# TensorE's matmuls in the program's order from the first step on, in a window-attention and Mish feed-forward kernel

## The chip, the cores and the metric

The kernel runs on one core of a Trainium2 chip. The metric is the device time of one execution in microseconds (us). Inputs and outputs are float32 in device memory.

## What is computed

Windowed attention over 8 sequences of 576 positions with 8 heads of 64, then a feed-forward layer whose activation is Mish, h * tanh(softplus(h)), on 4608 tokens of width 512 with an inner width of 2048:

```python
rel = pos[:, None] - pos[None, :]
mask = (rel >= 0) & (rel < 64)
scores = np.where(mask, scale * np.matmul(q, k.transpose(0, 1, 3, 2)), -1e9)
attn = np.exp(scores - np.max(scores, axis=-1, keepdims=True))
attn = attn / (np.sum(attn, axis=-1, keepdims=True) + 1e-09)
x = heads_side_by_side(np.matmul(attn, v))      # 4608 x 512
h = x @ w_in                                    # 512 x 2048
sp = np.where(h > 20.0, h, np.log1p(np.exp(np.minimum(h, 20.0))))
out = (h * np.tanh(sp)) @ w_out                 # 2048 x 512
```

## The kernel before

The 4608 tokens go in 12 chunks of 384 (`c`). A chunk's attention goes in four pairs of heads (`p`). Its feed-forward layer goes in 16 steps (`f`), each with 128 of the 2048 inner channels and its own weight tile.

**Attention of a pair.** `att_scores`: 12 small matmuls into two PSUM banks (`s_ps`); VectorE adds the mask and takes the row's extreme (L149), ScalarE takes the exponential (L152), VectorE scales by the sum (L160 to L162; in chunk 0 half by half, L156 to L158). `att_transpose`: six TensorE transposes of the probabilities `pr` into `t_ps` (L183), which are copied to `pT` (L184: by ScalarE, the second half by VectorE except in chunk 1). For chunks 4 and later VectorE and DMAs transpose instead, and TensorE has no part in it. `att_values`: 12 matmuls from `pT` into `o_ps`, whose result is split into a rounded part `xh` (ScalarE, L204) and the rest `xl` (VectorE, L205).

**A step.** `ffn_in`: 12 matmuls of 384 columns into `h_ps` (float32 products are built from rounded parts: xh and xl with the weight's high part, xh with its low part). VectorE clips (L223), ScalarE makes four passes (L224 to L231), VectorE combines with `h_ps` (L233), which frees the `h_ps` buffer (two exist). The result is split into `gh` (L235 or L237) and `gl` (GpSimd, L238). `ffn_out`, two steps later (`LAG`): 9 matmuls of 512 columns into three accumulators `acc`. The three accumulator banks (`ps_acc`) also hold `s_ps`, `t_ps` and `o_ps` of chunk 2's attention; other chunks mostly use three banks of their own (`bank`).

**Weights.** `load_w` fetches a step's weights as packed 64-bit words and takes them apart into float32 and then into a high and a low part: ScalarE L278, VectorE L279, L281, L282, L283, ScalarE L287, VectorE L288. There are two work buffers `wa`. A load's DMA waits until the tile three before it has been taken apart. All 16 tiles are taken apart once, while chunk 0 runs, and then stay.

**Order of the work.** The steps run (0, 0) to (0, 7), then chunks 0 and 1 in turns, then the rest of chunk 1, then chunk by chunk. Attention of chunk 0 comes first. Attention of a later chunk is spread over the steps before its own: `plan` gives each pair's scores, transposes and values a due time in half steps (`at`, `at + 0.6 * step`, `at + lag * step`), and the loop at L396 runs what is due (`run`) ahead of and behind each step's products. A scheduler then orders each engine's instructions by its own estimate of time and by priorities. `in_order()` takes part of that freedom away: inside it, every TensorE instruction that is traced is queued behind the last matmul recorded so far (`order[-1]`). It acts only once `ordered` holds something, which is from the first step of chunk 2 on (L401), and it is around the scores, the values and both products. The transposes are not recorded in `order` and are not inside it. On all engines the order is fixed when the program is built; at run time each engine takes its list from the top.

Of the kernel before, what the change touches and what calls it, by code (L numbers as in the profile page):

```python
# [27 lines left out]
def tile_window_attn_mish_ffn(  # L28
# [9 lines left out]
    nc = tc.nc  # L38
    NPAIR, _, NT = qT.shape
# [7 lines left out]
    NM = NB // 2  # L47
# [12 lines left out]
    ident = const.tile([P, P], F32, name="ident")  # L60
# [13 lines left out]
    for j in range(2):  # L74
        m = const.tile([P, P], F32, name=f"mask{j}")
# [15 lines left out]
    order = []  # L91
    ordered = []
# [4 lines left out]
    def in_order():  # L97
        return tc.issue_after(order[-1]) if ordered else nullcontext()
# [6 lines left out]
    def bank(c, p, name):  # L105
        if c == 2 or (c == 0 and p % 2 == 0):
            return ps_acc.tile([P, CH], F32, name=name, tag=next(sums))
        return ps_at.tile([P, CH], F32, name=name, tag="at")
# [56 lines left out]
    def att_transpose(c, p, pr):  # L165
        pT = next(pTs)
        if c > 3:


            moved = []  # L170
            tr = ap_.tile([P, P // 32, HM, 32], F32, name="tr", tag="pr", bufs=2)
            nc.vector.transpose(tr.rearrange("p k j i -> p j k i"),
                                pr.rearrange("p j (k i) -> p j k i", i=32))
            for r in range(0, P, 32):
                for k in range(0, P, 32):
                    if 0 <= k - r % BLK <= BLK:
                        moved.append(nc.sync.dma_start(pT[k:k + 32, r // 32, :, :], tr[r:r + 32, k // 32, :, :]))
            return pT, moved
        for h in range(2):
            t_ps = (bank(c, p, "t_ps") if c else ps_h.tile([P, CH], F32, name="t_ps", tag="h_ps")  # L180
                    ).rearrange("p (m k) -> p m k", k=P)
            for m in range(NM):
                nc.tensor.transpose(t_ps[:, m, :], pr[:, h * NM + m, :], ident)  # L183
            (nc.scalar.copy if h == 0 or c == 1 else nc.vector.tensor_copy)(  # L184
                pT[:, :, h * NM:(h + 1) * NM, :].rearrange("p r m i -> p m r i"),
                t_ps.rearrange("p m (r i) -> p m r i", i=32))
        return pT, []
# [19 lines left out]
    def ffn_in(c, x, f, alone=False):  # L207
        xh, xl = x
        h_ps = ps_h.tile([P, CH], F32, name="h_ps", tag="h_ps")
        n = 0  # L210
        for cc in range(NC_):
            for part, xx in ((0, xh), (0, xl), (1, xh)):
                pe(h_ps, ws[f][:, 0, part, cc * P:(cc + 1) * P], xx[:, cc, :],
                   start=n == 0, stop=n == 3 * NC_ - 1)
                n += 1
        t = mp.tile([P, CH], F32, name="t", tag="t", bufs=4)
        gh = mp.tile([P, CH], F32R, name="gh", bufs=3)
        gl = mp.tile([P, CH], F32R, name="gl", bufs=3)

        h = h_ps  # L220

        with tc.high_priority(offset=SOON):
            nc.vector.tensor_scalar(t, h_ps, 20.0, None, ALU.min)  # L223
            nc.scalar.activation(t, t, AF.Exp)  # L224
            if alone:

                h = ap_.tile([P, CH], F32, name="h", tag="pr", bufs=2)
                nc.scalar.copy(h, h_ps)
            nc.scalar.activation(t, t, AF.Square, bias=one_b)  # L229
            nc.scalar.activation(t, t, AF.Ln, bias=half_b, scale=0.5)  # L230
            nc.scalar.activation(t, t, AF.Exp, scale=-1.0)  # L231

            nc.vector.scalar_tensor_tensor(t, t, -1.0, h, ALU.add, ALU.mult)  # L233
            if c == 0:
                nc.scalar.copy(gh, t)  # L235
            else:
                nc.gpsimd.tensor_scalar(gh, t, 1.0, 0.0, ALU.mult, ALU.add)  # L237
            nc.gpsimd.tensor_tensor(gl, t, gh.bitcast(F32), ALU.subtract)  # L238
        return gh, gl
# [51 lines left out]
    class Att:  # L291
# [20 lines left out]
            self.load(p + 2, "qk")  # L312

        def transpose(self, p):
            with self.early():
                self.pT[p] = att_transpose(self.c, p, self.pr.pop(p))

        def values(self, p):
# [3 lines left out]
                att_values(self.c, p, self.v[p], self.pT.pop(p), self.x)  # L322
            self.load(p + 2, "v")

        def plan(self, begin, step, lag=1):

            for p in range(NPAIR):
                at = begin + p * step
                events.extend([(at, 2, self.scores, p), (at + 0.6 * step, 1, self.transpose, p),
                               (at + lag * step, 0, self.values, p)])  # L330

    events = []

    def run(slot):
        while events and events[0][0] <= slot:
            _, _, fn, p = events.pop(0)
            fn(p)
# [4 lines left out]
    def flush():  # L342
        c, f, gg = pend.pop(0)
        if f == 0:
            if c == 1:
                accs[c] = [ps_at.tile([P, DO], F32, name=f"acc1_{t}", tag="at") for t in range(NTT)]
            else:
                accs[c] = [ps_acc.tile([P, DO], F32, name=f"acc{t}", tag=f"acc{t}") for t in range(NTT)]
        ffn_out(accs[c], gg, f)
        if f == NF - 1:  # L350
            ffn_store(c, accs.pop(c))
# [3 lines left out]
    def take_w():  # L355
        if todo_w:
            load_w(todo_w.pop(0))
# [8 lines left out]
    third = 2 * len(steps) + 2  # L366
    steps += [(1, f) for f in range(NF - HEAD, NF)]
    starts = {c: 2 * len(steps) + 2 * NF * (c - 2) for c in range(2, NCHUNK)}
    steps += [(c, f) for c in range(2, NCHUNK) for f in range(NF)]

    atts = [Att(c) for c in range(NCHUNK)]
# [12 lines left out]
        if at == p and p != 1:  # L384
            take_w()
    atts[1].plan(0, 2 * HEAD / (NPAIR + 1))
    atts[2].plan(third, (starts[2] - third) / (NPAIR + 1), 1.5)


    ahead = 6  # L390
    begin = starts[2] + ahead + 1
    for c in range(3, NCHUNK):
        atts[c].plan(begin, (starts[c] - ahead - begin) / NPAIR)
        begin = starts[c] - ahead
    events.sort(key=lambda e: e[:2])
    for n, (c, f) in enumerate(steps):  # L396
        if f == 0:

            while any(fn.__self__ is atts[c] for _, _, fn, _ in events):
                run(events[0][0])  # L400
        if c == 2 and f == 0:  # L401
            ordered.append(True)
        with in_order():
            pend.append((c, f, ffn_in(c, atts[c].x, f, c == NCHUNK - 1)))
        run(2 * n)
        if len(pend) > LAG:
            with in_order():
                flush()
        run(2 * n + 1)
        if c == 0:  # L410
            take_w()
# [38 lines left out]
```

## Time and profile before

| | us |
|---|---|
| Median of 3 runs | 980.82 |
| Lowest and highest run | 979.62, 981.58 |
| The profiled execution | 980.18 |
| Its span (first to last instruction) | 978.4 |
| Mean granted TensorE clock | 0.983 |

Engines are PE (TensorE matmuls), PEld (TensorE weight loads), DVE (VectorE), ACT (ScalarE), POOL (GpSimd) and SP (SyncE, which issues the DMAs). In a row of the order of time the columns are start, duration, engine, line, operation, written tile and read tiles, shapes and count; in brackets stands how long the engine idled before it and what ended that. Rows of stages give the stage, its length, each engine's busy time with its count of instructions, the granted clock (1.00 is full speed), the DMA engines' busy share and GB/s. What the profile shows of the stages is quoted in the prediction.

### The profile page before, as it was taken

Reading aid. Unit: us, or ns where it says so; the run is one execution under the profiler, and the core shown is the slowest. Engines: PE = TensorE matmul, PEld = TensorE weight load, DVE = VectorE, ACT = ScalarE, POOL = GpSimd, SP = SyncE. Lnnn points to the kernel's source line nnn. Section 1 sums busy time; section 2 is a strip of 40 time slices with the busy share of each in tenths; the row PEclk is TensorE's granted clock in tenths of the full one; section 3 lists DMA queues with packets and bytes.
Section 4 is the critical chain, followed back from the end, with each engine's and each line's share of the span. In section 5 each row is a group of like instructions: output and inputs, shape, how many; then the busy total and the mean of one; then the engine's idle time right before and its main releaser. Section 6 shows DMA issues by size and latency. Waiting matters only on the chain.

```text
span 978.4 us, 17835 instructions
## 1 busy us (share of the span) xinstructions
PE 930.0 (95%) x6432; PEld 822.6 (84%) x6432; DVE 482.0 (49%) x1300; ACT 623.4 (64%) x1501; POOL 294.4 (30%) x387
## 2 busy tenths in 40 slices
PE   4688699998999999999999999999999999999997
PEld 3477599887888898888889888898898888889996
DVE  6999922443454544544544453544444454453222
ACT  5688756665666665665766756666666666665664
POOL 1013033321333333333333323333333333333333
PEclk9979899998999999999999999999999999999999
DMA  9655300122121311312311312312322322210000
GB/s 311 231 196 178 110 1 1 51 68 82 52 68 46 114 53 52 113 52 53 113 51 54 113 50 55 108 54 57 96 64 57 89 73 55 84 28 13 33 1 33
DMA packets 78040, 76.15 MB, mean 78 GB/s; under 512 B 9344, under 2 KB 71296, under 8 KB 75904
## 3 DMA queue, kind: packets, MB, share of 16 engines
q1 hardware_dynamic: 77952, 75.01, 25.0%
q8 instruction: 51, 0.84, 0.4%
q14 instruction: 37, 0.30, 0.1%
HBM read 56.10 MB, written 9.44 MB: 67 GB/s over the span
## 4 chain that ended last, share of the span: by engine, by line
PE 87%; DVE 10%; issue 1%; DMA 1%; ACT 1%; SPq 1%; ACTq 0%; POOL 0%; DVEq 0%; POOLq 0%
PE h_ps L95 40%; PE acc L95 39%; PE s_ps L95 4%; PE o_ps L95 4%; DVE w L288 2%; DVE wa L283 2%; DVE wa L282 1%; DVE wa L279 1%; DMA st<-w 1%; DVE pr L149 1%; PE t_ps L183 1%; DVE wa L281 1%; DVE t L223 1%; DVE t L233 0%; DVE xl L205 0%
## 5 line engine op out<-in xcount | busy, mean ns | idle before, releaser
L95 PE MATMUL h_ps<-xh,w 128*128 128x384 f32 x1536 | 431.3, 341 | 13.5 <-DVE t L233 11.8
L95 PE MATMUL acc<-w,gh 128*128 128x512 f32 x1152 | 343.1, 396 | 0.5 <-POOL gh L237 0.5
L95 PEld LDWEIGHTS h_ps<-xh,w 128*128 128x128 f32 x1536 | 284.8, 190 | 24.8 <-DVE t L233 13.6
L224 ACT ACTIVATE t<-t 128x384 f32<-128x384 f32 x192 | 100.6, 525 | 284.9 <-DVE t L223 284.6
L95 PE MATMUL h_ps<-xl,w 128*128 128x384 f32 x768 | 260.5, 339 | 0.8 <-DVE xl L205 0.8
L237 POOL TENSOR_SCALAR gh<-t 128x384 fp32r<-128x384 f32 x176 | 90.1, 512 | 551.6 <-DVE t L233 532.0
L95 PEld LDWEIGHTS acc<-w,gh 128*128 128x128 f32 x1152 | 211.2, 188 | 38.7 <-issue 5.8
L238 POOL TENSOR_TENSOR gl<-t,gh 128x384 fp32r<-128x384 f32 x192 | 200.1, 1042 | 125.7 <-ACT gh L235 92.1
L233 DVE SCALAR_TENSOR_TENSOR t<-t,h_ps 128x384 f32<-128x384 f32 x176 | 97.2, 553 | 256.4 <-ACT t L231 251.5
L95 PE MATMUL acc<-w,gl 128*128 128x512 f32 x576 | 205.4, 391 | 0.0
L95 PEld LDWEIGHTS h_ps<-xl,w 128*128 128x128 f32 x768 | 146.3, 190 | 8.3 <-DVE xl L205 1.1
L223 DVE TENSOR_SCALAR t<-h_ps 128x384 f32<-128x384 f32 x192 | 106.3, 555 | 77.4 <-PE h_ps L95 75.3
L95 PEld LDWEIGHTS acc<-w,gl 128*128 128x128 f32 x576 | 108.1, 188 | 24.2
L230 ACT ACTIVATE t<-t,half_b 128x384 f32<-128x384 f32 x192 | 118.3, 617 | 5.8
L229 ACT ACTIVATE t<-t,one_b 128x384 f32<-128x384 f32 x192 | 118.2, 617 | 4.4
L152 ACT ACTIVATE pr<-pr,mx 128x128 f32<-128x128 f32 x288 | 111.5, 389 | 14.8 <-DVE mx L149 14.7
L231 ACT ACTIVATE t<-t 128x384 f32<-128x384 f32 x192 | 100.1, 522 | 4.5
L149 DVE CUSTOM_DVE_ANT_0 pr<-s_ps,mask 128x128 f32<-128x128 f32 x288 | 64.9, 285 | 13.5 <-PE s_ps L95 13.5
L95 PEld LDWEIGHTS o_ps<-pT,v_t 128*64 128x64 f32 x1152 | 42.0, 145 | 23.0 <-issue 9.9
L95 PE MATMUL o_ps<-pT,v_t 128*64 128x64 f32 x1152 | 50.3, 234 | 8.3 <-DVE pT L184 5.4
L95 PE MATMUL s_ps<-k_t,q_t 64*64 64x128 f32 x1152 | 51.5, 295 | 4.5 <-DMA k_t<-kT 4.3
L152 ACT ACTIVATION_READ_ACCUMULATOR pr<-pr,mx 128x1 f32 x288 | 54.1, 188 | 0.0
(42 smaller groups left out, 432.6 us busy)
## 6 DMA issues: line engine op xcount, KB each, us to landing
v_t<-vN SPq DMA_DIRECT2D x48, 384.0 KB, 3.6
st<-w SPq DMA_DIRECT2D x16, 1024.0 KB, 5.0
k_t<-kT SPq DMA_DIRECT2D x47, 224.0 KB, 3.8
out<-o SPq DMA_DIRECT2D x36, 256.0 KB, 2.4
pT<-tr SPq DMA_DIRECT2D x384, 24.0 KB, 1.8
q_t<-qT SPq DMA_DIRECT2D x47, 192.0 KB, 3.9
q_t<-qT SPq DMA_DIRECT2D x3, 64.0 KB, 2.2
k_t<-kT SPq DMA_DIRECT2D x2, 64.0 KB, 2.0
```

Source lines behind the costliest of these rows:

```text
L95: order.append(nc.tensor.matmul(*args, **kw).ins)
L149: nc.vector.tensor_tensor_reduce(out=pr[:, j, :], in0=s_ps[h][:, m, :], in1=mk, op0=ALU.add, op1=ALU.min, scale=-0.125, scalar=3.0e38, acc ...
L152: nc.scalar.activation(pr[:, j, :], pr[:, j, :], AF.Exp, bias=mx[:, j:j + 1], scale=-1.0, accum_out=sm[:, j:j + 1])
L223: nc.vector.tensor_scalar(t, h_ps, 20.0, None, ALU.min)
L224: nc.scalar.activation(t, t, AF.Exp)
L229: nc.scalar.activation(t, t, AF.Square, bias=one_b)
L230: nc.scalar.activation(t, t, AF.Ln, bias=half_b, scale=0.5)
L231: nc.scalar.activation(t, t, AF.Exp, scale=-1.0)
L233: nc.vector.scalar_tensor_tensor(t, t, -1.0, h, ALU.add, ALU.mult)
L237: nc.gpsimd.tensor_scalar(gh, t, 1.0, 0.0, ALU.mult, ALU.add)
L238: nc.gpsimd.tensor_tensor(gl, t, gh.bitcast(F32), ALU.subtract)
L283: used.append(nc.vector.scalar_tensor_tensor(a, lo, 29, a, ALU.logical_shift_right, ALU.bitwise_or))
```

## The change

Transposes on TensorE are now recorded in `order` and stand inside `in_order()`. `ordered` is filled ahead of the first step, so that the order holds from there on. `plan` gets the transposes' place as an argument, `turn`, and for chunk 2 it goes from 0.6 to 1 step behind the scores. Attention of chunk 0 is traced before `ordered` is filled and stays free.

```diff
             for m in range(NM):
-                nc.tensor.transpose(t_ps[:, m, :], pr[:, h * NM + m, :], ident)
+                order.append(nc.tensor.transpose(t_ps[:, m, :], pr[:, h * NM + m, :], ident).ins)
...
         def transpose(self, p):
-            with self.early():
+            with in_order(), self.early():
                 self.pT[p] = att_transpose(self.c, p, self.pr.pop(p))
...
-        def plan(self, begin, step, lag=1):
+        def plan(self, begin, step, turn=0.6, lag=1):
...
-                events.extend([(at, 2, self.scores, p), (at + 0.6 * step, 1, self.transpose, p),
+                events.extend([(at, 2, self.scores, p), (at + turn * step, 1, self.transpose, p),
                                (at + lag * step, 0, self.values, p)])
...
-    atts[2].plan(third, (starts[2] - third) / (NPAIR + 1), 1.5)
+    atts[2].plan(third, (starts[2] - third) / (NPAIR + 1), 1, 1.5)
...
     events.sort(key=lambda e: e[:2])
+    ordered.append(True)
     for n, (c, f) in enumerate(steps):
...
-        if c == 2 and f == 0:
-            ordered.append(True)
```

Three places show how the engines' lists change. First TensorE, at the transposes of chunk 1's last pair (`t_ps`; `xh_236`, `xl_237` are chunk 0's input, `xh_576`, `xl_577` chunk 1's, `acc_631` to `acc_633` chunk 0's sums). Before:

```order
L95 MATMUL acc_631<-w,gl 128x512
L95 MATMUL acc_632<-w,gl 128x512
L95 MATMUL acc_633<-w,gl 128x512
L183 MATMUL t_ps<-ident,pr 128x128 x6
L95 MATMUL o_ps<-pT_103,v_t 64x64 x12
L95 MATMUL h_ps<-xh_236,w 128x384
```

Now:

```order
L95 MATMUL h_ps<-xl_237,w 128x384
L95 MATMUL h_ps<-xh_236,w 128x384
L183 MATMUL t_ps<-ident,pr 128x128 x6
L95 MATMUL acc_631<-w,gh 128x512 x2
L95 MATMUL acc_631<-w,gl 128x512
L95 MATMUL acc_632<-w,gh 128x512 x2
L95 MATMUL acc_632<-w,gl 128x512
L95 MATMUL acc_633<-w,gh 128x512 x2
L95 MATMUL acc_633<-w,gl 128x512
L95 MATMUL o_ps<-pT_103,v_t 64x64 x12
L95 MATMUL h_ps<-xh_236,w 128x384
```

Counted from the start of the lists, these transposes had nine first products of chunk 0 and nine matmuls of chunk 1's first one ahead of them, and eight second products; now they have seven first products and four second ones ahead of them, all of chunk 0.

Second VectorE, at the end of the weight work. Before:

```order
L288 TENSOR_TENSOR w<-wa,w 128x2x512
L282 SCALAR_TENSOR_TENSOR wa<-st,wa 128x1024
L223 TENSOR_SCALAR t<-h_ps 128x384 x2
L279 TENSOR_SCALAR wa<-wa 128x1024
L283 SCALAR_TENSOR_TENSOR wa<-st,wa 128x1024
L281 TENSOR_SCALAR wa<-wa 128x1024
L282 SCALAR_TENSOR_TENSOR wa<-st,wa 128x1024
L288 TENSOR_TENSOR w<-wa,w 128x2x512
L283 SCALAR_TENSOR_TENSOR wa<-st,wa 128x1024
L233 SCALAR_TENSOR_TENSOR t<-t,h_ps 128x384 x2
L288 TENSOR_TENSOR w<-wa,w 128x2x512
```

Now:

```order
L288 TENSOR_TENSOR w<-wa,w 128x2x512
L233 SCALAR_TENSOR_TENSOR t<-t,h_ps 128x384
L282 SCALAR_TENSOR_TENSOR wa<-st,wa 128x1024
L223 TENSOR_SCALAR t<-h_ps 128x384
L160 TENSOR_SCALAR sm<-sm 128x6
L283 SCALAR_TENSOR_TENSOR wa<-st,wa 128x1024
L161 RECIPROCAL sm<-sm 128x6
L162 TENSOR_TENSOR pr<-pr,sm 128x768
L288 TENSOR_TENSOR w<-wa,w 128x2x512
L233 SCALAR_TENSOR_TENSOR t<-t,h_ps 128x384
L205 TENSOR_TENSOR xl_577<-o_ps,xh_576 128x384
```

The last pair's scaling (L160 to L162) has moved from some 18 rows ahead of the last L288 to the place just ahead of it. From the third xl of chunk 0 to the last L288 the list had eleven L223, eleven L233 and five L205, and now has seven, six and four; every other kind has the same count.

Third TensorE, just ahead of chunk 2's first product (`xh_1825`, `xl_1826` are its input, `acc_0_1172` to `acc_2_1174` chunk 1's sums). Before:

```order
L95 MATMUL acc_2_1174<-w,gl 128x512
L95 MATMUL s_ps<-k_t,q_t 64x128 x6
L183 MATMUL t_ps<-ident,pr 128x128 x6
L95 MATMUL s_ps<-k_t,q_t 64x128 x6
L95 MATMUL o_ps<-pT_102,v_t 64x64 x12
L183 MATMUL t_ps<-ident,pr 128x128 x6
L95 MATMUL o_ps<-pT_103,v_t 64x64 x12
L95 MATMUL h_ps<-xh_1825,w 128x384
```

Now:

```order
L95 MATMUL h_ps<-xh_576,w 128x384
L183 MATMUL t_ps<-ident,pr 128x128 x6
L95 MATMUL acc_0_1172<-w,gh 128x512 x2
L95 MATMUL acc_0_1172<-w,gl 128x512
L95 MATMUL acc_1_1173<-w,gh 128x512 x2
L95 MATMUL acc_1_1173<-w,gl 128x512
L95 MATMUL acc_2_1174<-w,gh 128x512 x2
L95 MATMUL acc_2_1174<-w,gl 128x512
L95 MATMUL o_ps<-pT_103,v_t 64x64 x12
L95 MATMUL h_ps<-xh_1825,w 128x384
```

Before, the last pairs' scores, transposes and values stood one behind the other with no product between; now products stand between a pair's scores and its transposes, and between these and its values. In three places of this stretch a pair's scores directly follow the transposes of the pair before.

## The prediction

> **What bounds the kernel now.** I read the page first (busy time, and the 40 slices), then busy time by stage, then the order of time on VectorE and TensorE in the stages that stand out. On the page:
>
> ```profile
> PE 930.0 (95%) x6432; PEld 822.6 (84%) x6432; DVE 482.0 (49%) x1300; ACT 623.4 (64%) x1501; POOL 294.4 (30%) x387
> ...
> PE   4688699998999999999999999999999999999997
> ...
> DVE  6999922443454544544544453544444454453222
> ```
>
> TensorE is full except in the first five slices (about 122 us), near 220 us, and in the last slice. Where TensorE has its gaps, VectorE is full. By stage (us, then busy time of PE, PEld, DVE, ACT, POOL, the granted clock, DMA):
>
> ```profile
> 41.30:126.00 84.70, 65.50 (x441) 55.78 (x439) 81.43 (x146) 63.97 (x138) 16.96 (x12) 0.86 0.49 163
> 126.00:202.00 76.00, 76.00 (x440) 68.21 (x438) 24.48 (x64) 47.84 (x98) 23.08 (x29) 1.00 0.05 17
> 202.00:262.00 60.00, 56.75 (x428) 49.51 (x427) 25.14 (x78) 34.65 (x94) 15.28 (x20) 0.94 0.22 69
> 262.00:979.00 717.00, 710.76 (x4914) 634.20 (x4912) 317.16 (x913) 452.92 (x1109) 234.91 (x308) 1.00 0.22 64
> ```
>
> So 41 to 126 us is VectorE's stage (81.4 of 84.7 us busy). Its groups between 41 and 124 us (count, busy us, mean ns, idle time before them) show what fills it, the taking apart of twelve weight tiles (L279 to L288), and that it idles only 0.5 + 0.9 + 0.2 us:
>
> ```profile
> L282 DVE SCALAR_TENSOR_TENSOR wa<-st,wa 128x1024 uint32<-128x1024 uint32 x12 | 15.4, 1287 | 0.0
> L288 DVE TENSOR_TENSOR w<-wa,w 128x1024 fp32r<-128x1024 f32 x12 | 15.4, 1285 | 0.2 <-ACT w L287 0.2
> L283 DVE SCALAR_TENSOR_TENSOR wa<-st,wa 128x1024 uint32<-128x1024 uint32 x12 | 15.4, 1285 | 0.0
> L279 DVE TENSOR_SCALAR wa<-wa 128x1024 f32<-128x1024 f32 x11 | 9.2, 835 | 0.5 <-ACT wa L278 0.5
> ...
> L149 DVE CUSTOM_DVE_ANT_0 pr<-s_ps,mask 128x128 f32<-128x128 f32 x24 | 5.6, 283 | 0.9 <-PE s_ps L95 0.9
> L162 DVE TENSOR_TENSOR pr<-pr,sm 128x768 f32<-128x768 f32 x4 | 3.8, 952 | 0.0
> ```
>
>  From 126 us TensorE sets the pace, with one dent between 202 and 262. Every us by which TensorE's list of work is behind when VectorE lets go of it is a us at the end. In the change's order TensorE's last 3873 of 5280 matmuls stand as they stood, so the 717 us behind 262 get no term. What remains is two places: the end of VectorE's weight work, and the dent.
>
> **Place one: where VectorE lets go of TensorE.** I call a pair's scores S, its transposes T, its values O; a step's first product H (12 matmuls), its second A (9). Before, TensorE's last hold is this one, and afterwards it runs full:
>
> ```profile
> 113.85 0.34 PE L95 MATMUL h_ps<-xh,w 128*128 128x384 f32 x1
> 122.45 0.69 PE L95 MATMUL h_ps<-xh,w 128*128 128x384 f32 x1 [8.27 <-DVE t L233]
> ```
>
> By the order, at 122.45 us TensorE has issued 11 H (ten of chunk 0, one of chunk 1), 9 A and all four S, T, O of chunk 1. In the changed order T of pair 3 cannot pass or be passed, and it has ahead of it only 7 H, 4 A, four S, three T and three O. Behind it remain, compared with before at 122.45 us, 4 H, 5 A, one T and one O. Their durations at full clock, H and A from the chain of waits, T and O from the two rows 220.84 and 222.75 further below:
>
> ```profile
> 132.88 2.11 PE h_ps L95 x12
> 134.98 2.06 PE acc L95 x9
> ```
>
> That is 4 x 2.11 + 5 x 2.06 + 0.87 + 0.92 = **20.5 us** of TensorE work.
>
> When can this T start? It reads pr, which VectorE writes in L162. In the new VectorE list L162 of pair 3 stands just ahead of the last weight instruction (L288), that is, at the end of the weight work. The new list up to there is the old list up to its last L288, less four L223, five L233 and one L205. Price of each from start to start, and the old end:
>
> ```profile
> 100.75 0.55 DVE L205 TENSOR_TENSOR xl<-o_ps,xh 128x384 fp32r<-128x384 f32 x1
> 101.22 0.55 DVE L223 TENSOR_SCALAR t<-h_ps 128x384 f32<-128x384 f32 x1
> 101.69 0.54 DVE L233 SCALAR_TENSOR_TENSOR t<-t,h_ps 128x384 f32<-128x384 f32 x1
> 102.15 1.22 DVE L283 SCALAR_TENSOR_TENSOR wa<-st,wa 128x1024 uint32<-128x1024 uint32 x1
> ...
> 123.05 1.23 DVE L288 TENSOR_TENSOR w<-wa,w 128x1024 fp32r<-128x1024 f32 x1 [0.19 <-ACT w L287]
> ```
>
> L205 0.47, L223 0.47, L233 0.46: together 4 x 0.47 + 5 x 0.46 + 0.47 = 4.65 us. From 123.05, less its wait of 0.19, this gives 118.2 us.
>
> One correction. Six of VectorE's instructions here are about 0.83 us longer than their kind (the first and the last below, with a usual L279), and each runs beside an L238 of GpSimd, of which nine start between 57.56 and 110.00:
>
> ```profile
> 57.56 1.06 POOL L238 TENSOR_TENSOR gl<-t,gh 128x384 fp32r<-128x384 f32 x1 [52.43 <-ACT gh L235]
> 58.84 1.47 POOL L238 TENSOR_TENSOR gl<-t,gh 128x384 fp32r<-128x384 f32 x1 [0.22 <-ACT gh L235]
> ...
> 110.00 1.21 POOL L238 TENSOR_TENSOR gl<-t,gh 128x384 fp32r<-128x384 f32 x1 [5.76 <-ACT gh L235]
> ```
>
> ```profile
> 59.36 2.03 DVE L288 TENSOR_TENSOR w<-wa,w 128x1024 fp32r<-128x1024 f32 x1
> ...
> 104.18 0.68 DVE L279 TENSOR_SCALAR wa<-wa 128x1024 f32<-128x1024 f32 x1
> ...
> 110.25 1.51 DVE L279 TENSOR_SCALAR wa<-wa 128x1024 f32<-128x1024 f32 x1
> ```
>
> The new list has six L233, so at most six L238, ahead of that L162: six of nine, so four long ones instead of six, 1.7 us less. I take **116.6 us** for the start of T of pair 3. Bounds: 118.2 if all six long ones stay; 112 if none stays (another 3.3) and the 1.4 us for which VectorE idled also goes; upwards 121 if new waits of about a us fall on VectorE at each of the four T.
>
> The Trainium skill ("SBUF — State Buffer", the list under its port diagram) says the port pair that VectorE and GpSimd share is an exclusive lock, the loser blocking for the whole instruction. By it the long ones go with the number of L238; if they went with elapsed time instead, the end would be 118.2.
>
> Does VectorE run through without waiting for the held TensorE? I laid its new list on time from 41.0 us with the durations above: L162 of the four pairs ends near 63, 82, 98 and 117 us. Behind each, TensorE has at most 2 H, 2 A, an S, an O and the T itself, 8 to 9 us, or 11 with half clock at the start, before the next T, against gaps of 16 to 19 us. So it stands before each T for 6 to 11 us, and VectorE's next L149 and L223 find their S and H done. Only ScalarE is tight (a rival).
>
> Head: 116.6 + 20.5 - 122.45 = **+14.7 us**. Both orders come out of a long hold with slow matmuls (0.69 above, against 0.34), so that cancels. The DMA queue sets no new bound: the last weight's load now stands behind one that waits for S of pair 2, near 90 us; it lands some 5 us later, and ScalarE takes it up near 106.
>
> ```profile
> st<-w SPq DMA_DIRECT2D x16, 1024.0 KB, 5.0
> ```
>
> The long hold at 122.45 goes; what is late next is T, four times.
>
> **Place two: the dent before chunk 2.**
>
> ```profile
> 220.03 0.87 PE L95 MATMUL s_ps<-k_t,q_t 64*64 64x128 f32 x12
> 220.84 0.87 PE L183 MATMUL t_ps<-ident,pr 128*128 128x128 f32 x6
> 221.95 0.87 PE L95 MATMUL s_ps<-k_t,q_t 64*64 64x128 f32 x12 [0.24 <-ACT pT L184]
> 222.75 0.92 PE L95 MATMUL o_ps<-pT,v_t 128*64 128x64 f32 x24
> 226.43 1.51 PE L183 MATMUL t_ps<-ident,pr 128*128 128x128 f32 x6 [2.76 <-DVE pr L162]
> ...
> 228.59 1.54 PE L95 MATMUL o_ps<-pT,v_t 128*64 128x64 f32 x22 [0.24 <-DVE pT L184]
> 230.07 0.69 PE L95 MATMUL h_ps<-xh,w 128*128 128x384 f32 x1
> ...
> 233.25 0.62 PE L95 MATMUL acc<-w,gh 128*128 128x512 f32 x2
> ```
>
> From 220.03 to 230.07 are 10.04 us for two half S, two T, two O, which at full clock are 2 x (0.87 + 0.87 + 0.92) = 5.3: 4.7 lost. The next H takes 3.18 instead of 2.11: 1.1 more. Lost: 5.8 us, of which 3.24 are waits and the rest slow clock. In the new order every T has 2 H or H and A's between it and its S (7 us for the last, against the 3.6 us from the end of S, 222.8, to T at 226.43), so the long wait goes. New: three times S follows T at once, and its second bank is T's first, still to be copied by ScalarE. The row at 221.95 prices that at 0.24; behind one more ScalarE instruction it would be near 0.9. I take 0.4 each, 1.2 in all: **-4.6 us**, bounds 0 and -5.8.
>
> The Trainium skill ("TensorE: Matmul & The Clock Gate", "Why this matters for your kernels") asks for idle gaps above about 3 us before the clock drops; here a wait of 2.76 us, with only small matmuls around it, is followed by T at 1.51 us instead of 0.87. By the rule only the 3.2 us of waits would go, and the sum would be 992.
>
> **Sum.** +14.7 - 4.6 = +10.1 on the profiled execution's 980.18 us (span 978.4 and 1.8 around it) is 990.3. That execution lies 0.64 us below the median of the three runs, 980.82. I say **990**.
>
> **Rivals.**
> - *ScalarE's queue passes the hold on to VectorE.* In the new order ScalarE's copies of T (L184) stand ahead of casts and absolutes of weights (L287, L278) that VectorE needs next. It happened before:
>
> ```profile
> 93.13 0.87 ACT L184 COPY pT<-t_ps 128x384 f32<-128x384 f32 x2 [2.97 <-PE t_ps L183]
> ```
>
> ```profile
> 95.05 0.69 DVE L279 TENSOR_SCALAR wa<-wa 128x1024 f32<-128x1024 f32 x1 [0.46 <-ACT wa L278]
> ```
>
> ```profile
> L278 ACT ACTIVATE wa<-st 128x1024 f32<-128x1024 f32 x11 | 12.8, 1160 | 5.6 <-DVE w L288 5.6
> ```
>
>   From L162 to ScalarE's next weight instruction: T at half clock 1.5, copies 0.9, the instruction 1.2, so 3.6 us, against 2.8 to 4 us of other work on VectorE. If it is late by 1 to 2 us at three holds: 993 to 996. Against: one copy or two, and the row costs only 0.46. 15%.
> - *The dent is not mended* (S behind T costs what the wait did): 980.2 + 14.7 = 995. 8%. *Half mended, the clock drop stays*: 992 to 993. 6%.
> - *Fewer long instructions still*: all gone, T at 112 to 113, 986. 5%.
> - *Faster: VectorE, rid of ten instructions, frees TensorE early.* The hold of 8.27 us and the dent are gone for good, and this wins if the last T starts before 122.45 - 20.5 + 4.6 = 106.5 us; at 100 it would give 974. For: VectorE alone sets that time, and its weight work is unchanged. Against: the list ends 10 us later, and even without long ones and idle time at 112. 3%.
> - *No change*: the held work would have to be hidden elsewhere, but from 126 us TensorE has no idle time to hide it in. 2%.
>
> **How the numbers follow.** The forecast's own case (VectorE full, T held four times, dent mostly mended: 987 to 993) has 61%. The range takes in the 986 and 996 cases and the bounds of T's start (112 to 121, so -5 and +4): **984 to 998**. A measurement of this kernel tells about 0.2% (2 us) from no change. Faster 3%, same 2%, slower 95%.
>
> **What would show it.** Right: TensorE waits for L162 four times between 50 and 118 us with some 30 us in total, the wait for L233 of 8.27 us is gone, the last L288 starts near 117, TensorE is full from there to the dent, and near 225 us no wait above 1 us. Wrong: VectorE idle by several us between 41 and 118 (ScalarE rival), a weight finished before 112, waits for ScalarE's copies at S of chunk 2, or idle time behind 262 us, which the sum leaves out.

## The result and the profile after

The changed kernel takes 987.7 us (median of 4 runs, 986.94 to 988.59), the kernel before in the same comparison 981.03 us (979.62 to 981.58). The ratio is 1.0071, with a 95% interval of 1.0053 to 1.0088: slower by 6.7 us. The profiled execution of the changed kernel took 988.1 us, with a span of 986.3 us against 978.4 before.

By stage (us, then busy time of PE, PEld, DVE, ACT, POOL, the granted clock, DMA), the changed kernel, in the stages that were shown of before:

```profile
41.30:126.00 84.70, 50.01 (x382) 43.27 (x383) 77.83 (x140) 57.17 (x119) 10.75 (x7) 0.78 0.48 166
126.00:202.00 76.00, 76.00 (x394) 68.73 (x394) 21.42 (x43) 47.17 (x85) 22.39 (x27) 1.00 0.03 11
202.00:262.00 60.00, 60.00 (x467) 52.41 (x464) 28.34 (x102) 40.14 (x115) 18.11 (x23) 1.00 0.24 76
```

TensorE has lost 15.5 us of busy time ahead of 126 us (65.5 before, and part of the 50.0 is at a lower clock), and the dent between 202 and 262 us is gone. What TensorE waits for from 41 to 130 us, the line that leads the view of waits before, and then the first and the last line of the same view now:

```profile
PE h_ps L95 <- DVE t L233: 11.8, 5, 8.3
```

```profile
PE t_ps L183 <- DVE pr L162: 32.5, 4, 11.2
...
PE h_ps L95 <- DVE xl L205: 0.4, 1, 0.4
```

No wait for L233 is left. The order of time on TensorE has the four waits:

```profile
63.34 1.51 PE L183 MATMUL t_ps<-ident,pr 128*128 128x128 f32 x6 [11.22 <-DVE pr L162]
...
82.25 1.51 PE L183 MATMUL t_ps<-ident,pr 128*128 128x128 f32 x6 [7.72 <-DVE pr L162]
...
98.37 1.51 PE L183 MATMUL t_ps<-ident,pr 128*128 128x128 f32 x6 [5.80 <-DVE pr L162]
...
116.90 1.51 PE L183 MATMUL t_ps<-ident,pr 128*128 128x128 f32 x6 [7.73 <-DVE pr L162]
```

And the order of time on VectorE has what they waited for, the last L162 just ahead of the last L288:

```profile
62.24 0.95 DVE L162 TENSOR_TENSOR pr<-pr,sm 128x768 f32<-128x768 f32 x1
...
81.16 0.95 DVE L162 TENSOR_TENSOR pr<-pr,sm 128x768 f32<-128x768 f32 x1
...
97.27 0.95 DVE L162 TENSOR_TENSOR pr<-pr,sm 128x768 f32<-128x768 f32 x1
...
115.79 0.96 DVE L162 TENSOR_TENSOR pr<-pr,sm 128x768 f32<-128x768 f32 x1
116.77 1.23 DVE L288 TENSOR_TENSOR w<-wa,w 128x1024 fp32r<-128x1024 f32 x1
117.91 0.55 DVE L233 SCALAR_TENSOR_TENSOR t<-t,h_ps 128x384 f32<-128x384 f32 x1
```

Between 41 and 118 us VectorE's groups (count, busy us, mean ns, idle time before them) show that it did not idle while TensorE stood:

```profile
L282 DVE SCALAR_TENSOR_TENSOR wa<-st,wa 128x1024 uint32<-128x1024 uint32 x12 | 16.9, 1411 | 0.1
L288 DVE TENSOR_TENSOR w<-wa,w 128x1024 fp32r<-128x1024 f32 x13 | 15.7, 1211 | 0.0
L283 DVE SCALAR_TENSOR_TENSOR wa<-st,wa 128x1024 uint32<-128x1024 uint32 x12 | 14.6, 1214 | 0.0
```

In the dent's place TensorE runs through. Three of chunk 2's four S now run whole, each right behind a T, and TensorE does not idle there:

```profile
208.72 0.82 PE L183 MATMUL t_ps<-ident,pr 128*128 128x128 f32 x6
209.46 1.18 PE L95 MATMUL s_ps<-k_t,q_t 64*64 64x128 f32 x24
210.58 0.45 PE L95 MATMUL h_ps<-xh,w 128*128 128x384 f32 x1
...
236.54 0.82 PE L183 MATMUL t_ps<-ident,pr 128*128 128x128 f32 x6
...
239.37 0.92 PE L95 MATMUL o_ps<-pT,v_t 128*64 128x64 f32 x24
```

**Where the time went.** A clean mark in every trace is the VectorE instruction at L261 that takes a third of a chunk's sums out of PSUM, once a chunk, right behind the chunk's last second product. Of the kernel before and of the changed one, for chunks 0 and 1 (order of time):

```profile
182.46 0.69 DVE L261 TENSOR_SCALAR o<-acc 128x512 f32<-128x512 f32 x1 [0.97 <-PE acc L95]
...
239.00 0.69 DVE L261 TENSOR_SCALAR o<-acc 128x512 f32<-128x512 f32 x1 [0.74 <-PE acc L95]
```

```profile
198.10 0.69 DVE L261 TENSOR_SCALAR o<-acc 128x512 f32<-128x512 f32 x1 [0.97 <-PE acc L95]
...
248.15 0.69 DVE L261 TENSOR_SCALAR o<-acc 128x512 f32<-128x512 f32 x1 [0.74 <-PE acc L95]
```

At the end of chunk 0 the changed kernel is 15.6 us late, at the end of chunk 1 (the dent lies between) 9.15 us. The same mark in chunk 2 is at 320.24 and 328.52, 8.3 us late; in the last chunk at 973.79 and 981.71, 7.9 us late. So: head +15.6, dent -6.5, chunk 3's attention (which runs in chunk 2) -0.9, later -0.4.

### The profile page after: what moved, and what is told of

Read it like the earlier page. It is cut to its first block, busy times and chain, and to the rows that moved or that the text cites. A ratio compares the mean times of both kernels' runs of the same rounds, so it can differ in the third digit from the quotient of the medians.

```text
span 986.3 us, 17843 instructions
## 1 busy us (share of the span) xinstructions
PE 924.5 (94%) x6432; PEld 819.8 (83%) x6432; DVE 482.5 (49%) x1300; ACT 625.8 (63%) x1501; POOL 293.4 (30%) x387
## 4 chain that ended last, share of the span: by engine, by line
PE 87%; DVE 9%; issue 1%; DMA 1%; SPq 1%; ACT 0%; ACTq 0%; POOL 0%; DVEq 0%; POOLq 0%
PE acc L95 40%; PE h_ps L95 40%; PE o_ps L95 4%; PE s_ps L95 3%; DVE wa L282 2%; DVE w L288 1%; DVE wa L283 1%; DVE wa L279 1%; DMA st<-w 1%; DVE wa L281 1%; PE t_ps L183 1%; DVE pr L149 1%; DVE t L223 0%; DVE pr L162 0%; DVE t L233 0%
## 5 line engine op out<-in xcount | busy, mean ns | idle before, releaser
L95 PE MATMUL acc<-w,gh 128*128 128x512 f32 x1152 | 346.8, 399 | 0.5 <-POOL gh L237 0.5
L238 POOL TENSOR_TENSOR gl<-t,gh 128x384 fp32r<-128x384 f32 x192 | 199.1, 1037 | 153.6 <-ACT gh L235 139.0
L233 DVE SCALAR_TENSOR_TENSOR t<-t,h_ps 128x384 f32<-128x384 f32 x176 | 97.4, 553 | 269.8 <-ACT t L231 264.8
L223 DVE TENSOR_SCALAR t<-h_ps 128x384 f32<-128x384 f32 x192 | 106.6, 555 | 78.1 <-PE h_ps L95 73.3
L149 DVE CUSTOM_DVE_ANT_0 pr<-s_ps,mask 128x128 f32<-128x128 f32 x288 | 64.5, 285 | 7.3 <-PE s_ps L95 7.3
L95 PEld LDWEIGHTS o_ps<-pT,v_t 128*64 128x64 f32 x1152 | 40.9, 145 | 23.9 <-issue 11.6
L183 PE MATMUL t_ps<-ident,pr 128*128 128x128 f32 x96 | 19.6, 350 | 42.3 <-DVE pr L162 32.5
L95 PE MATMUL o_ps<-pT,v_t 128*64 128x64 f32 x1152 | 48.3, 235 | 9.5 <-DVE pT L184 8.0
```

Source lines behind the costliest of these rows:

```text
L95: order.append(nc.tensor.matmul(*args, **kw).ins)
L149: nc.vector.tensor_tensor_reduce(out=pr[:, j, :], in0=s_ps[h][:, m, :], in1=mk, op0=ALU.add, op1=ALU.min, scale=-0.125, scalar=3.0e38, acc ...
L183: order.append(nc.tensor.transpose(t_ps[:, m, :], pr[:, h * NM + m, :], ident).ins)
```

## The experiments

My theory: TensorE cannot pass a T, T waits for L162, L162 stands deep in VectorE's full list, and the products behind T are what is lost. The rivals: that the held transposes are the cause as such, that any strict order costs in the head, that the order costs in every chunk. Times are medians. The kernel before took 980.69 us beside the runs e1 to e4 (marked in the table) and 981.12 us beside the other four experiments. The last column of this table is from the L261 marks of each one's profiled execution.

| Run | Median us | Ratio to before (95% interval) | Late against before at the end of chunk 0, 1, 11 |
|---|---|---|---|
| changed kernel | 987.7 | 1.0071 (1.0053 to 1.0088) | +15.6, +9.2, +7.9 |
| order from step (1, 8) on (e1) | 974.76 | 0.9943 (0.9928 to 0.9958) | +1.9, -4.6, -4.6 |
| the same, chunk 2's T at 0.6 | 973.58 | 0.9926 (0.9909 to 0.9943) | +1.8, -4.1, -4.7 |
| the same, T free | 975.62 | 0.9951 (0.9934 to 0.9967) | +2.8, -1.6, -1.0 |
| order from the start, T free (e2) | 985.53 | 1.0053 (1.0038 to 1.0068) | +9.0, +4.6, +4.8 |
| chunk 1's T at 1.0 | 976.52 | 0.9951 (0.9937 to 0.9966) | +4.2, -2.3, -3.2 |
| chunk 1's T at 1.6 (e3) | 965.93 | 0.9853 (0.9837 to 0.9869) | -6.3, -12.8, -13.1 |
| chunk 1's T at 1.9, pairs closer | 963.89 | 0.9825 (0.9809 to 0.9841) | -8.8, -15.3, -15.5 |
| changed, L238 twice in chunk 0 (e4) | 991.69 | 1.0115 (1.0100 to 1.0130) | +18.9, +11.4, +10.5 |

**Order only behind the weights (e1).** Against the changed kernel:

```diff
-    ordered.append(True)
     for n, (c, f) in enumerate(steps):
+        if (c, f) == (1, NF - HEAD):
+            ordered.append(True)
```

> The changed kernel, but the order holds only from the step (1, 8) on, when all weights have been taken apart; ahead of it the lists of TensorE and VectorE are those of before. My theory (the loss sits ahead of 126 us, where TensorE waits for L162 behind VectorE's weight work, and the dent ahead of chunk 2 is a gain of 6.5 us with 0.9 us more in chunk 3): TensorE waits for L162 ahead of 126 us 3.8 us in total as before, no dent near 226 us, 981.0 - 7.4 = 973.6 us, between 972.5 and 975. Rival (the order costs something in every chunk, and the two traces only happen to agree behind chunk 3): 980 us or more.

974.76 us. TensorE's waits for L162 ahead of 130 us are 3.7 us, as before, and none follows. Between the ends of chunks 0 and 1 it gains 6.5 us on before (+1.9 to -4.6), the same as the changed kernel. The loss is in the head, the gain in the dent, and the two are separate. The median is inside the stated 972.5 to 975.

One reading has to be taken with care: its head ends 1.9 us later than before's, with lists that are the same up to there. In before's profiled execution VectorE waits 0.46 and 0.86 us at L279 and L149 near 95 us; here the same two instructions wait longer:

```profile
95.95 0.69 DVE L279 TENSOR_SCALAR wa<-wa 128x1024 f32<-128x1024 f32 x1 [1.05 <-ACT wa L278]
97.92 0.29 DVE L149 CUSTOM_DVE_ANT_0 pr<-s_ps,mask 128x128 f32<-128x128 f32 x1 [1.28 <-PE s_ps L95]
```

Three executions with this head list (this one and the two below that also hold the order only from step (1, 8) on) end chunk 0 at 184.2 to 185.3 us, before's profiled one at 182.5. TensorE's clock differs between them. By stage (us, TensorE's busy time, the granted clock, DMA), before near 90 us and behind its last hold, then the same two places here:

```profile
88.90:92.30 3.40, 3.40 (x11) 0.50 0.83 294
122.45:126.40 3.95, 3.94 (x12) 0.50 0.00 0
```

```profile
88.20:95.00 6.80, 6.11 (x20) 0.50 0.42 154
123.76:129.20 5.44, 5.44 (x17) 0.50 0.00 0
```

The half clock lasts 3.4 us near 90 us in before's execution and 6.8 us in each of the three, and 4.0 us behind the last hold against 5.4. That is nearly 2 us of the difference; the latest of the three was another 0.9 us late already at 16 us. With the same list, a head's length so scatters by 2 to 3 us from one execution to the next, and part of the +15.6 above is such scatter. By the medians it is about one us: before's profiled execution lies 0.85 us below its median and the changed kernel's 0.4 us above its own, which is the difference between the medians' 6.7 us and the spans' 7.9. The last column of the table has the same scatter: the profiled executions of the two other runs with the order from step (1, 8) on lie 2.0 and 3.6 us above their medians.

**The transposes free, the rest in order from the start (e2).**

```diff
-                order.append(nc.tensor.transpose(t_ps[:, m, :], pr[:, h * NM + m, :], ident).ins)
+                nc.tensor.transpose(t_ps[:, m, :], pr[:, h * NM + m, :], ident)
...
-            with in_order(), self.early():
+            with self.early():
                 self.pT[p] = att_transpose(self.c, p, self.pr.pop(p))
```

> The changed kernel with the transposes free again; scores, values and products stay in the program's order from the first step on. My theory (values and the next pair's scores stand behind the transposes by their data, so TensorE is held just as well; T of the last pair can start when the VectorE list reaches its L162, 67.2 us of work behind 41.4, with four long instructions 112 us, and 4 H, 4 A, a T and an O, 18.4 us, are behind): head +8, dent mended -6.5: 982 to 984 us, waits for L162 still above 20 us ahead of 126 us. Rival (it is the held transposes themselves): these waits fall to about 4 us and the time to 973 to 975.

985.53 us, 1.5 above the range that I gave. TensorE's order of time shows it held at every T as well, in sum 14.9 us, where above 20 us were expected. For two of the four the view names another releaser than L162, but L162 ends only 0.14 us ahead of T there (at 93.07 and 111.92 us):

```profile
63.28 1.51 PE L183 MATMUL t_ps<-ident,pr 128*128 128x128 f32 x6 [3.19 <-DVE pr L162]
...
78.21 0.84 PE L183 MATMUL t_ps<-ident,pr 128*128 128x128 f32 x6 [2.67 <-DVE pr L162]
...
93.21 1.03 PE L183 MATMUL t_ps<-ident,pr 128*128 128x128 f32 x6 [3.19 <-ACT gh L235]
...
112.06 1.51 PE L183 MATMUL t_ps<-ident,pr 128*128 128x128 f32 x6 [5.80 <-ACT t L229]
```

The last T starts at 112.06, the 112 that was worked out, and the head costs 9.0 us for 8 expected. Freeing T takes back less than half of the head's loss. My reading of the rest is that the values and the next pair's scores, which are in the order, stand behind T, and the products behind them. Two thirds of the miss in the total are the dent, which gives only 4.4 us here (9.0 to 4.6) where I had counted 6.5; the other us is the head.

**Chunk 1's transposes later (e3, then 1.0 and 1.9).** Three places for the same pairs, with the order held from the first step as in the changed kernel:

```diff
-    atts[1].plan(0, 2 * HEAD / (NPAIR + 1))
+    atts[1].plan(0, 2 * HEAD / (NPAIR + 1), 1.6, 1.9)
```

> The changed kernel with chunk 1's transposes 1.6 and its values 1.9 steps behind the scores instead of 0.6 and 1. My theory (what costs is only that products stand behind a T whose L162 comes late; with one or two products more ahead of each T, VectorE's list reaches L162 of the last pair at 50.6 instead of 70.6 us of work and twelve instead of six steps' L233 stand ahead of the last L288): the four waits for L162 fall from 32.5 to below 10 us in total, the head costs between -5 and +2 us against before, the dent stays mended: 969 to 976 us, 972 likeliest. Rival (an order that TensorE cannot leave costs in the head wherever the transposes stand, because VectorE is full there): 983 us or more.

965.93 us, below the range that I gave. Ahead of 130 us no wait for L162 is left. What TensorE waits for most there is L233, which frees the buffers of the first product:

```profile
PE h_ps L95 <- DVE t L233: 11.6, 5, 4.2
```

A strict order need not cost anything in the head: it ends 6.3 us earlier than before's, where I had expected -5 to +2. No run has these later places without the order, so it stays open how much of this gain is the order's and how much the places'. The list has two more first products ahead of T of pair 0 than the changed kernel's (four for two), and eight for seven ahead of the last.

The place in between, with `1.0, 1.3`:

> The changed kernel with chunk 1's transposes 1.0 and its values 1.3 steps behind the scores, between 0.6 (987.7 us) and 1.6 (965.9 us). VectorE's list reaches the last pair's L162 after 60.5 us of work (70.6 and 50.6), and eight L233 stand ahead of its last L288 (six and twelve). Theory (the loss goes with the products that stand behind the held T, 4.2 us for each step): the waits for L162 ahead of 126 us are between 8 and 20 us, 977 to 983 us. Rival (a threshold: any place behind the scores that lets one product more stand ahead is enough): 968 us or less.

976.52 us, just under the range. The waits for L162 lie in between as well:

```profile
PE t_ps L183 <- DVE pr L162: 12.6, 4, 3.7
```

No threshold: 32.5 us, 12.6 us and no wait for L162, and 987.7, 976.5 and 965.9 us. A place later still, with the pairs closer together, `plan(0, 2 * HEAD / (NPAIR + 1.5), 1.9, 2.3)`:

> The changed kernel with chunk 1's pairs 2.9 instead of 3.2 half steps apart, transposes 1.9 and values 2.3 of these behind the scores. VectorE's list reaches the last pair's L162 after 47.3 us of work, with five L233 ahead of it, and 13 L233 stand ahead of the last L288 (six and twelve with transposes 1.6 behind). Theory (what counts is how many steps VectorE has served by the end of its weight work): as good as the run with 1.6 or one to two us better, 964 to 966 us. Rival (there is an optimum in the place, past it values and the next chunk's first products come late): 968 us or more.

963.89 us, 0.1 below the stated range and 1.75% below before, the fastest version here. TensorE's stage from 41 to 126 us:

```profile
41.30:126.00 84.70, 72.90 (x505) 62.45 (x506) 83.88 (x149) 69.84 (x147) 20.77 (x14) 0.96 0.48 163
```

VectorE is as full as before (83.9 of 84.7 us; 81.4 before), TensorE has 72.9 us of work done where before had 65.5 and the changed kernel 50.0, and the clock is 0.96 instead of 0.86 and 0.78. VectorE's work is the same; what it does first has changed. The last 2 us do not come from products ahead of T: each T has as many first and second products ahead of it as with 1.6 (four, five, seven and eight first ones). TensorE's waits for L233 ahead of 130 us are shorter, 10.2 us with 2.6 for the longest instead of 11.6 and 4.2, and its clock from 41 to 126 us is 0.96 instead of 0.94.

**Which part mends the dent.** The order from step (1, 8) on, with chunk 2's transposes left at 0.6:

> As the run with the order from step (1, 8) on, but chunk 2's transposes stay 0.6 steps behind the scores instead of 1. Theory (the dent goes because products stand between S and T; with 0.6 there are still 3.9 to 5 us of products and values between them, and T followed S by 3.6 us in the dent of before): dent mended as well, no wait of T for L162 above 0.7 us behind 130 us, 974 to 976 us. Rival (it is the later place, not the order, that mends the dent): waits of T for L162 of 1 us or more come back, 978 us or more.

973.58 us, just below the stated range: from the end of chunk 0 to that of chunk 1 it gains 5.8 us on before (50.7 us for 56.5), and no wait for L162 is left behind 130 us. The order mends the dent; the later place adds 0.7 us by the marks, and the medians (974.76 and 973.58) do not show it. And with the transposes free:

> As the run with the order from step (1, 8) on, but transposes are free. Theory, from the end of each chunk in the runs so far: with free transposes the dent gives 4.4 instead of 6.5 us and chunk 3's 0.9 us stay away, so 2 to 3 us more than the run with the order from (1, 8) on: 976 to 978 us. Rival (the order of scores, values and products mends all of it): 974 to 975 us.

975.62 us, a little below the stated range. In the profiled execution the dent gives 4.4 us, as it did with free transposes from the start, and chunk 3 gives nothing: the order of scores, values and products mends two thirds, the transposes' place in it the rest. Three of the four S are cut in two here, as they were before. The medians (974.76 and 975.62, intervals that overlap) do not tell the two apart; the marks in the traces do.

**GpSimd's subtraction twice (e4).**

```diff
-            nc.gpsimd.tensor_tensor(gl, t, gh.bitcast(F32), ALU.subtract)
+            [nc.gpsimd.tensor_tensor(gl, t, gh.bitcast(F32), ALU.subtract) for _ in range(1 + (c == 0))]
```

> The changed kernel with GpSimd's subtraction L238 made twice in every step of chunk 0 (the second writes the same values). VectorE's list up to the last L162 of chunk 1 has the same instructions in sum. My theory (a GpSimd L238 beside a busy VectorE lengthens one VectorE instruction by about 0.83 us in two cases of three): six more L238 ahead of T of the last pair make three to six more long instructions; that T moves from 116.9 to between 119 and 122 us, and the whole to 990 to 993 us. Rival (the long instructions have another cause and only fall beside L238 by chance): T at 117 us, 987.5 us, the number of VectorE instructions that are 0.3 us or more above their kind stays near six.

991.69 us, as expected. Counting, in the order of time on VectorE between 41 us and the last L288, the instructions that are over 0.25 us longer than their kind gives six in the changed kernel, 4.1 us in sum, and twelve here, 8.7 us in sum. The first two of the twelve, beside GpSimd's two:

```profile
56.67 1.48 DVE L281 TENSOR_SCALAR wa<-wa 128x1024 uint32<-128x1024 uint32 x1
58.08 0.96 DVE L160 TENSOR_SCALAR sm<-sm 128x6 f32<-128x6 f32 x1
```

```profile
56.58 2.42 POOL L238 TENSOR_TENSOR gl<-t,gh 128x384 fp32r<-128x384 f32 x2 [51.45 <-ACT gh L235]
```

Each of them runs beside an L238. The last T moves from 116.90 to 120.89 us. So the long instructions are L238's doing, one each, and nearly all of their 4.6 us more reaches TensorE (4.0 us) while VectorE sets the pace. The Trainium skill ("SBUF — State Buffer", the list under its port diagram) has the shared port pair as an exclusive lock held for a whole instruction; the trace agrees. Each of the eighteen long instructions (six and twelve) is longer than its kind by what was left of the L238 at its start, less 0.14 us. In the changed kernel the L160 at 114.04, with 0.46 us left, takes 0.49 instead of 0.17 us, and the L281 at 57.23, with 0.94 left, is 0.80 longer:

```profile
113.19 1.31 POOL L238 TENSOR_TENSOR gl<-t,gh 128x384 fp32r<-128x384 f32 x1 [9.63 <-ACT gh L235]
```

```profile
114.04 0.49 DVE L160 TENSOR_SCALAR sm<-sm 128x6 f32<-128x6 f32 x1
```

## Why the prediction came out right, step by step

- *VectorE's stage sets the head: right.* Its list ran with under 0.2 us of idle time, so laying the new list end to end gave the right times: the four L162 end near 63.2, 82.1, 98.2 and 116.8 us, for 63, 82, 98 and 117.
- *T of the last pair starts at 116.6: right*, 116.90. One correction in it was off: six L238 were expected to lengthen four instructions, and lengthened six, by 0.7 instead of 0.83 on average (4.1 us for 3.3). VectorE's idle time of before, 1.4 us, went, which I had kept in the sum and named in the bounds. And the changed kernel's execution was 0.46 us late by the end of chunk 0's attention, ahead of any change (its last T there starts at 36.66 us, before's at 36.20). These errors partly cancel, so that the hit to 0.3 us is in part luck.
- *20.5 us of products behind that T, head +14.7: right.* It measured +15.6 in the profiled pair, and 12.8 to 13.9 against the three executions of before's head list in e1 and the two runs like it. In the profiled pair 0.3 us of the 0.9 more is T's start. The rest is about what the half clock behind the two holds makes, which I had let cancel: it lasts 5.8 us from T at 116.90 on, and 4.0 us from 122.45 on before.
- *The dent gives 4.6: too small*, it gave 6.5, outside my bound of 5.8. Most of the miss is one size: I priced the S by halves, as before had them. A half takes 0.81 us from start to start (220.03 to 220.84, 221.95 to 222.75), but a whole one takes hardly more where nothing holds it up, as chunk 2's first S of before:

```profile
186.97 0.89 PE L95 MATMUL s_ps<-k_t,q_t 64*64 64x128 f32 x24
187.79 0.44 PE L95 MATMUL h_ps<-xh,w 128*128 128x384 f32 x1
```

  So a cut S costs 0.8 us more. Before cut three of the four, the new order cuts one, and 1.6 us were not in the sum. The 1.2 us that I charged for three S behind a T came, only smaller: these three take 1.12 us (209.46 to 210.58), 0.3 more each. The first half starts at once, so TensorE shows no idle time, but the second starts at 209.78, when ScalarE has just copied T's first half (to 209.72):

```profile
209.24 0.48 ACT L184 COPY pT<-t_ps 128x384 f32<-128x384 f32 x1 [0.55 <-PE t_ps L183]
```

  The 5.8 us that before had lost, 1.6 for the cuts, less 0.9 for the copies, are the 6.5 measured.
- *No term behind 262 us: wrong by 0.9 us.* The 3873 matmuls that stand as they stood begin only at 297.05 us of before, behind chunk 3's last transposes. These moved with the order, and chunk 2 gained 0.87 us. In both runs with free transposes this gain is absent.
- *Rivals.* ScalarE's queue did not pass the hold on (VectorE idle under 0.2 us). The clock did not stay low in the dent's place. The sum, +10.1, is 2.2 above the profiled pair's +7.9: the dent gave 1.9 more, chunk 3 0.9 and a later stretch 0.4, against a head that cost 0.9 more.

The first run with free transposes and the three places of T bear out the cause and not only the sum: the loss follows the products behind the held T, and goes to nothing and below as more of them stand ahead. With each place L162 also moves forward in VectorE's list, and no run separates the two.

## What to carry to other kernels

Before an engine is given a fixed order, find the engine that is full in that stage and ask at which place of its list each waited-for result stands; an instruction that waits in a fixed order costs the work queued behind it. Then choose the place of the waiting instruction, not only the order: here the same order was 6.7 us slower or 17 us faster by the place of one chunk's transposes and values in it. Lay the full engine's list end to end with measured durations; here that gave the start of the last transpose to 0.3 us, with single errors of up to 1.4 us that partly cancelled.

## What was unexpected of the hardware

- In the traces' record the granted clock is 1.0 or 0.5 in all ten profiles, and its changes lie whole multiples of 3.41 us apart (before: 41.1, 51.4, 61.6, 88.9, 92.3, 116.2, 126.4, 225.4, 232.3 and 976.4 us). So it depends on where a wait falls whose work the half clock meets. Before, T behind 2.76 us at 226.43 took 1.51 us, as the clock had dropped at 225.4. In e2 T behind 2.67 us at 78.21 took 0.84, and the clock dropped at 80.1, behind it, for 3.4 us. The Trainium skill ("TensorE: Matmul & The Clock Gate", "Why this matters for your kernels") draws the line for an idle gap at about 3 us. Here the clock dropped during a wait of 2.76 us in one place and 1.9 us after the end of one of 2.67 us in the other, and the dent, which gave 6.5 us where the waits alone were 3.2, speaks for the row and against the rule.
- L238 lengthened VectorE's instructions by 0.3 to 0.8 us, that is, by what was left of the L238, and whatever the instruction's own size: also a 128x6 one that usually takes 0.17 us (0.96 in e4 at 58.08).
- The 24 records of scores take 0.82 us whole (186.97 before) and 2 x 0.81 us when something stands between the halves: 12 of them are hardly faster than 24.
